# A block of linear attention and a gated feed-forward on one core: the first two token tiles get k and v by direct products, and the schedule's model and order are drawn up anew

## The chip, the cores and the metric

The kernel runs on one core of a Trainium2 chip. The metric is device microseconds of one execution. Of the engines, TensorE is called PE below, VectorE DVE, ScalarE ACT, GpSimd POOL, and SP is the queue that issues nearly all DMAs.

## The reference

`x` has 2048 tokens of 512 elements. It is normalised per token (mean and variance). On the result `xn` two things are computed and multiplied:

```python
qkv = xn @ wqkv                                  # 32 heads of 16
pq, pk = q @ w_phi, k @ w_phi                    # per head, 16 x 16
phi = concat(softmax(p), softmax(-p))            # for q and for k
kv, z = phi_k^T @ v, sum over tokens of phi_k    # per head
s = (phi_q @ kv) / (phi_q . z + 1e-6) @ wo
h = xn @ w1 + b1                                 # 512 -> 1792
g = silu(mish(h) @ w2)                           # 1792 -> 512
out = x + s * g
```

## The kernel before

Tokens are handled in 16 tiles of 128; two tiles form a pair `c` (0 to 7). Every value is float32. A matmul takes each operand as a high half (rounded, written by ACT) and a low half (the rest, by DVE or POOL), so one product costs three matmuls per 128 rows of depth: `lo x hi`, `hi x lo`, `hi x hi`. With 256 rows, a product (`blocks`) is six matmuls.

The large products are cut into 2 x 2 blocks and done with seven block products in place of eight (`SUMS`, `kv_a` to `kv_d`, `q_proj`, `product`). For k and v of a pair, the left blocks are the two tiles and the two halves of the 512 features, the right blocks are k weights and v weights. The seven products need sums and differences of the blocks on both sides: of x (`xs`, split into `fh`/`fl` numbers 107 to 114 for pairs 0 to 3) and of the weights (`ws2`, `ws3`, `ws4` and the `wk` halves). Products of one pair are added in the PSUM tiles `kx`, `kz`, `ky`, and DVE adds the parts in SBUF (`plus`). The k weights are first folded with `w_phi` on PE (`fold`, tiles `wkf`); the same is done for q (`wqf`).

The parts of the program, by the letter that stands in `ORDER`: `N` a tile's normalisation and transposition (`pt`), `Ka` to `Kd` k and v of a pair with the softmax, `A` the sum over tokens (`kvp`, 64 narrow matmuls of a pair), `P` and `M` the weights w1 (prepared and written to DRAM; read back as `w1b`), `F` the first feed-forward product, `L` the reading back of x blocks of the second half (`fh`, `fl` from `xd`), `Q` q, `D` the denominators, `U` the numerators (`pn`), `O` wo, `R` w2, `G` the second feed-forward product (`y`), `E` and `H` the end. Small letters are weights: `wv`, `wq`, `wo`, and `kl`, `ks`, `kd`, `k4` (in the change also `kh`) the parts of the k weights and their sums with those of v. In `D`, `ez` and `tz` are the products with the sum of phi_k and their sums; `put` writes a part of the hidden layer to DRAM (`hd`).

The order on PE is that of `ORDER`. The order on the other engines and on SP comes from a simulation in the kernel's own Python code (`Program.simulate`): it walks through time with a cost per operation, gives every ready operation to a free engine by due time, and holds back those that find no free buffer. There are 38 large buffers (`SLOTS`), 15 small ones (`S2`) and 8 PSUM banks. All instructions are recorded by one helper and so have one line in the profile, L371.

At the start PE runs 13 matmuls on ones (`wake`), and then waits for the first tokens.

Of the kernel before, what the change touches and what calls it, by code (L numbers as in the profile page):

```python
# [23 lines left out]
FC = F // P  # L24
NB = FC // 2
NQ = NT // 2
DIRECT = 0
NC = 8
PEN, HOLD, MARGIN, GUARD = 0, 300, 1000, 140
BACK, COLD, DRATE, LANES, SWITCH = 1500, 3400, 400, 8, 300  # L30
BLOCK, HEAD, FETCH, IDLE = 256, 89, 5200, 2100
BEGIN = {"PE": 1100, "V": 900, "G": 2300, "A": 800, "Q": 800}

# [1 line left out]
SLACK, AHEAD, LAT = 15000, 40000, 150  # L35
WAKE, EACH, NEAR = 13, 2, 4000
ORDER = """
N0 kl wv1 wv0 kd N2 N1 N8 Ka1 wq0 N3 Ka4 ks N9 N6 k4 N7 Ka0 N4 Kb0 N5 Kc0 Kd0 Ka3 Kb1 N10 Kc1 P0 N11 Kb3 Kd1 Ka5 b1
Ka2 A0 Kb2 Kc2 Kc3 A1 Kd2 Fa0 Kd3 Fb0 Fc0 Kb5 N14 Kc5 P4 Kb4 A2 Fa4 Fd0 Kc4 N12 Kd4 N13 P3 N15 Kd5 A3 Fb4 Ka6 Fc4 Ka7
Kb7 Kc7 Kb6 Kc6 Fd4 P2 Fa3 Fb3 wq1 P5 Kd7 Kd6 Fa2 A4 Fa5 Fc3 Fb2 Fc2 P1 Fd3 A5 A6 wQ Fb5 Fc5 Q0 P6 A7 Fd5 Q1 z Fa6 D0  # L40
D1 Fd2 Fa1 Fb1 Fb6 Fc1 D2 Q3 Q2 L M4 Fa11 M5 D3 Fc6 D4 M3 D5 D6 Fb11 Fd1 Fa10 Fc11 Fd6 Q5 Q4 Fb10 Fc10 Fd11 wo1 M6 D8
Fd10 D7 D9 Fa12 M1 Fb12 Fa8 Fc12 Fa13 Fd12 D10 Q7 Fb13 D11 Fb8 Fc13 M0 Ub0 Fc8 Fd13 Fd8 wo0 Q6 Fa7 Ua0 Fb7 M2 Fa9 D12
Fc7 Fb9 D13 O2 O1 Fd7 Fc9 O6 O7 O0 O3 D14 D15 O4 R0 Ub1 R1 Fd9 O5 Ua1 G7 R2 G8 O11 O8 G9 R4 R5 O10 G0 R3 G1 G2 G10 R6
G3 G4 G5 G11 G12 G13 E1 G6 O9 G35 E0 O13 G36 O15 O12 G37 O14 G38 G28 G29 G30 G39 G31 G32 G40 H1 G41 E5 G33 G34 G21 G22
G23 E4 G24 H5 G25 G26 G27 E3 G42 G43 G14 G15 G16 H0 G17 H3 G44 G18 G45 G19 G20 G46 G47 G48 E6 H6 H4 E2 G49 H2 E7
"""
ACT_SET = {AF.Exp: 1, AF.Silu: 3, AF.Mish: 2}

# [5 lines left out]
class Program:  # L54
# [8 lines left out]
    @staticmethod  # L63
    def cost(e, m, a, k):
        aps = [v for v in a if isinstance(v, bass.AP)]
        n = aps[0].free_size()
        if e == "PE":
            if m == "transpose":
                return 109
            n, c = aps[2].free_size(), aps[1].free_size()  # L70
            if aps[1].dtype == F32R:
                return max(n / 2.4 + 0.104 * c, c * 0.835 + 2)
            full = 2 * max(n / 1.2 + 2.5, c * 0.835)
            if aps[1].shape[0] == 32:
                return max(0.146 * n, 24)
            return max(full * aps[0].shape[0] / P, 27)
        if e == "Q":
            return 450
        if e == "A":
            return (60 if aps[1].space == "PSUM" else 110) + 0.833 * n + 93 * sum(isinstance(v, bass.AP) for v in k.values())  # L80
        psum = any(v.space == "PSUM" for v in aps[1:])
        nn = max(v.free_size() for v in aps)
        if e == "V":
            if m == "reciprocal":
                return 70 + 6.3 * n
            if m in ("tensor_scalar", "tensor_copy") and not psum:
                return 70 + 0.52 * n
# [104 lines left out]
    def simulate(self, at):  # L192
# [49 lines left out]
        def go(o, e):  # L242
            nonlocal aset, dma, half, code, fetched, cold
            dur, calls = o.impl[e]
            if e == "A":
                for s in o.sets:
                    if s != aset:
                        dur += 1283
                        aset = s
            if e == "PE":  # L250
                if now > busy["PE"] + IDLE or pe[0].start is None:
                    cold = now + COLD
                if now < cold:
# [12 lines left out]
            if e in o.lock:
                port["V"], port["G"] = now + dur, now + dur + (GUARD if e == "V" else 0)
            o.start, o.eng = now, e
            for n in o.new:
                free[self.tag[n]] -= 1  # L270
                want[self.tag[n]].remove(n)
            busy[e] = now + dur
            end = now + dur + (200 if e == "PE" else 140)
            if e == "Q":
                if not lanes:
                    dur = 0
                    busy[e] = now
                dma = max(dma, now + (1100 if now > 2500 else 1350)) + volume(calls[0][1]) / DRATE
                end = dma + 1150
                lanes.append(end)  # L280
                heapq.heappush(events, (dma - BACK, 2, -1))
            for s in o.succ:
                s.open -= 1
                s.soon = max(s.soon, end)
                if s.open == 0 and s.ndep > 0 and len(s.impl) == 1 and "PE" not in s.impl:
                    for e2 in s.impl:
                        soon[e2].append(s)
            heapq.heappush(events, (now + dur, 2, -1))
            heapq.heappush(events, (end, 1, o.idx))
# [8 lines left out]
        while left:  # L298
# [8 lines left out]
            for kind, i in todo:  # L307
# [6 lines left out]
                elif kind == 1:  # L314
                    o = ops[i]
                    left -= 1
                    for n in o.tiles:
                        if n in uses:
                            uses[n] -= 1
                            if uses[n] == 0:  # L320
                                free[self.tag[n]] += 1
                    for s in o.succ:
                        s.ndep -= 1
                        if s.ndep == 0:
                            s.ready = now
                            if "PE" not in s.impl:
                                for e in s.impl:
                                    heapq.heappush(ready[e], (s.late + (PEN if e == "V" and len(s.impl) > 1 else 0), s.idx))
# [60 lines left out]
def volume(aps):  # L389

    runs = []
    for v in aps[:2]:
# [22 lines left out]
def block_kernel(ctx: ExitStack, tc: tile.TileContext, x, wqkT, wv, phi, wo, w1, b1, w2, out):  # L415
# [120 lines left out]


    xd = dram.tile([P, 2, 7, 2, 4, P], F32, name="xd")
    xc, pts, tiles, fx = {}, {}, {}, {}
# [29 lines left out]
    def norm(t):  # L569
# [25 lines left out]
        split(pt[:, 2:4], *xc[c][2])  # L595
        x12 = alloc("s2", [P, 2, P], f"xr{c}")
        d = slot([P, 4, 2, P], f"xs{c}")
        copy(x12, pt[:, 0:2])
        for i, a, b in ((0, x12, p0[:, 0:2]), (1, pt[:, 2:4], d[:, 0]), (2, pt[:, 2:4], x12), (3, p0[:, 2:4], d[:, 1])):
            V.tensor_tensor(d[:, i], a, b, op=ALU.subtract)  # L600
# [33 lines left out]
    def plus(t, ps):  # L634
        V.tensor_tensor(t, t, ps, op=ALU.add)

    def blocks(ps, lhs, rhs, first):
        with one():
            for k in range(2):
                (ah, al), (bh, bl) = lhs(k), rhs(k)  # L640
                for i, (u, v) in enumerate(((al, bh), (ah, bl), (ah, bh))):
                    PE.matmul(ps, u, v, start=first and k == 0 and i == 0, stop=k == 1 and i == 2, skip_group_check=True)

    kvp = bank([P, 4, 64], "kvp")
    zacc = slot([P, 2 * D], "zacc")
# [5 lines left out]
    def k_soft(t, p, ps):  # L651
# [2 lines left out]
        scale(e, r)  # L654
        ek[t] = e.rearrange("p h s d -> p (h s d)")

    def kv_a(c):
        x, z = bank([P, D], f"kx{c}"), bank([P, D], f"kz{c}")
        v0 = vs[2 * c] = s2(f"v{2 * c}")
        kv_mm(x, c, 0, 0, True)  # L660
# [3 lines left out]
        kv[c] = x  # L664

    def kv_b(c):
        x, y, k1 = kv[c], bank([P, D], f"ky{c}"), s2(f"k{2 * c + 1}p")
        v1 = vs[2 * c + 1] = s2(f"v{2 * c + 1}")
        kv_mm(x, c, 4, 4, False)
# [3 lines left out]
        kv[c] = x, y, k1  # L673

    def kv_c(c):
        x, y, k1 = kv[c]
        kv_mm(x, c, 5, 5, False)
        plus(k1, x)
# [357 lines left out]
    def low_k():  # L1036
        wkv[2] = halves("wk", 1)
        for j in range(2):
            split(fold(wkT, "wk", 2 + j), *(t[:, j] for t in wkv[2]))

    def diff_k():
        t = slot([P, 2, D], "ws3")
        for j in range(2):
            V.tensor_tensor(t[:, j], wraw["v", 0][:, j], fold(wkT, "wk", j), op=ALU.subtract)
        wkv[5] = split_raw(t, "ws3")

    def last_k():
        t = slot([P, 2, D], "ws4")
# [36 lines left out]
    def sums():  # L1085
# [16 lines left out]
        for i in range(4):  # L1102
# [3 lines left out]
    wqT = [None] * KC  # L1106
    wkT = load_wT(KC, "wk", 0, 2) + load_wT(KC, "wk", 1, 2)
    parts = {"b1": bias, "z": sums,
             "ks": sum_k, "kl": low_k, "kd": diff_k, "k4": last_k, "wv": weights_v, "wq": weights_q, "wQ": sums_q, "wo": weights_o, "N": norm, "Ka": kv_a, "Kb": kv_b, "Kc": kv_c, "Kd": kv_d, "A": kv_acc, "Q": q_proj, "D": den, "Ua": num_a, "Ub": num_b,
             "O": att_out, "L": load_g, "P": prep1, "M": again1, "R": prep2,  # L1110
             "Fa": ffn1a, "Fb": ffn1b, "Fc": ffn1c, "Fd": ffn1d, "G": ffn2, "E": final, "H": gate}
    for c in ORDER.split():
# [36 lines left out]
```

## Time and profile before

| what | value |
|---|---|
| median of 3 runs | 502.48 us (501.42 to 505.03) |
| the profiled execution | 501.77 us, span 499.9 us |
| PE busy | 485.1 us, 97%, 3842 matmuls |
| DVE, ACT, POOL busy | 456.0, 287.3, 266.2 us |
| granted PE clock, mean | 0.999 |
| DMA | 105.70 MB, 211 GB/s |

A profile is read from the whole to the piece: busy shares of the engines, then the same by stretches of time, then what the engine that is the bound has waited for, and the chain of work that ended last, in order of time. Names stand as out<-in; in those views the number behind a name is left out, in the order below it is kept.

### The profile page before, as it was taken

To read this page: it belongs to the slowest core of one execution; us is meant where nothing else is said; L and a number is where in the kernel's file an instruction comes from. 1 tells how busy PE (TensorE), PEld (TensorE's weight loads), DVE (VectorE), ACT (ScalarE), POOL (GpSimd) and SP (SyncE) were. 2 spreads that over 40 slices of the span, in tenths; PEclk is the share of its full clock that TensorE was granted. 3 is DMA by queue.
4 is the path that set the end of the run, shared out by engine and by line. 5 is a ranking of instruction groups with operands and counts; after the bars stand their busy time and mean duration, and the time that the engine had idled before them with its cause. 6 is when DMAs were issued, how large, how long until landed. Compare 5 with 4: busy or idle time off the path is not lost.

```text
span 499.9 us, 10373 instructions
## 1 busy us (share of the span) xinstructions
PE 485.1 (97%) x3842; PEld 428.0 (86%) x3842; DVE 456.0 (91%) x883; ACT 287.3 (57%) x440; POOL 266.2 (53%) x199
## 2 busy tenths in 40 slices
PE   6889999999999999998999999999999999999996
PEld 6778888888878979787887888788998999999996
DVE  5999999989899999988988989979998999998985
ACT  3887625564456373332533564587669686876731
POOL 2678999799791567877876398370003403220001
PEclk9999999999999999999999999999999999999999
DMA  8534444368987569997683945573437555676442
GB/s 290 183 109 148 179 129 134 128 224 281 345 329 278 211 215 302 370 366 272 201 272 129 313 150 197 207 234 106 128 115 262 200 171 197 211 258 208 158 140 107
DMA packets 68642, 105.70 MB, mean 211 GB/s; under 512 B 6896, under 2 KB 37744, under 8 KB 68592
## 3 DMA queue, kind: packets, MB, share of 16 engines
q1 hardware_dynamic: 68448, 104.79, 61.4%
q8 instruction: 30, 0.49, 0.4%
q10 hardware_dynamic: 144, 0.26, 0.1%
q14 instruction: 20, 0.16, 0.1%
HBM read 60.60 MB, written 44.43 MB: 210 GB/s over the span
## 4 chain that ended last, share of the span: by engine, by line
PE 82%; DMA 7%; DVE 7%; issue 2%; ACT 1%; POOL 1%; SPq 0%; DVEq 0%; POOLq 0%
PE y L371 21%; PE fx L371 15%; PE pw L371 9%; PE kx L371 9%; PE fy L371 7%; PE ky L371 4%; PE fz L371 4%; PE qx L371 3%; PE pn L371 2%; DMA r<-hd 2%; DMA fl<-xd 2%; PE kz L371 2%; DVE al L371 2%; DMA w1b<-w1d 2%; PE kvp L371 2%
## 5 line engine op out<-in xcount | busy, mean ns | idle before, releaser
L371 ACT ACTIVATE ah<-r 128x896 fp32r<-128x896 f32 x56 | 51.2, 944 | 13.7 <-DVE r L371 9.7
L371 DVE TENSOR_TENSOR al<-r,ah 128x896 fp32r<-128x896 f32 x48 | 52.6, 1123 | 3.0 <-ACT ah L371 2.4
L371 DVE TENSOR_TENSOR r<-r 128x128 f32<-128x128 f32 (+1 forms) x151 | 48.2, 365 | 4.2 <-ACT r L371 3.6
L371 PE MATMUL y<-w2h,al 128*128 128x256 f32 x160 | 45.5, 284 | 0.7 <-DVE yc L371 0.7
L371 PE MATMUL y<-w2h,ah 128*128 128x256 f32 x160 | 45.3, 283 | 0.0
L371 PE MATMUL y<-w2l,ah 128*128 128x256 f32 x160 | 45.3, 283 | 0.0
L371 POOL TENSOR_TENSOR r<-r 128x128 f32<-128x128 f32 (+1 forms) x17 | 9.4, 560 | 63.0 <-DVE r L371 51.2
L371 ACT ACTIVATE r<-r 128x512 f32<-128x512 f32 x56 | 33.6, 624 | 14.7 <-DMA r<-hd 14.3
L371 PE MATMUL y<-w2t,ah 128*128 128x256 f32 x224 | 40.9, 283 | 0.0
L371 PE MATMUL fx<-fh,w1b 128*128 128x512 f32 x112 | 38.9, 394 | 1.3 <-DMA w1b<-w1d 1.3
L371 PEld LDWEIGHTS y<-w2t,ah 128*128 128x128 f32 x224 | 34.9, 192 | 0.0
L371 PEld LDWEIGHTS y<-w2h,al 128*128 128x128 f32 x160 | 30.7, 192 | 1.5 <-DVE yc L371 0.9
L371 PE MATMUL y<-w2t,al 128*128 128x256 f32 x112 | 31.7, 283 | 0.0
L371 PEld LDWEIGHTS y<-w2l,ah 128*128 128x128 f32 x160 | 30.7, 192 | 0.2
L371 PEld LDWEIGHTS y<-w2h,ah 128*128 128x128 f32 x160 | 30.7, 192 | 0.0
L371 PE MATMUL y<-w2g,ah 128*128 128x256 f32 x160 | 30.4, 283 | 0.0
L371 POOL TENSOR_TENSOR xx<-sr,xx 128x512 f32<-128x512 f32 x3 | 3.9, 1299 | 47.7 <-DVE sr L371 41.9
L371 POOL TENSOR_TENSOR al<-r,ah 128x896 fp32r<-128x896 f32 x8 | 17.0, 2130 | 22.7 <-DVE sr L371 18.6
L371 PEld LDWEIGHTS fx<-fh,w1b 128*128 128x128 f32 x112 | 21.0, 188 | 7.0 <-DMA w1b<-w1d 1.5
L371 PEld LDWEIGHTS y<-w2g,ah 128*128 128x128 f32 x160 | 24.9, 192 | 0.0
L371 PE MATMUL y<-w2g,al 128*128 128x256 f32 x80 | 22.6, 283 | 0.0
L371 ACT ACT_TABLE_LOAD x13 | 16.7, 1283 | 9.3 <-DVE yy L371 5.2
(728 smaller groups left out, 1749.7 us busy)
## 6 DMA issues: line engine op xcount, KB each, us to landing
r<-hd SPq DMA_DIRECT2D x56, 256.0 KB, 4.1
xd<-xc SPq DMA_DIRECT2D x8, 896.0 KB, 4.4
w1b<-w1d SPq DMA_DIRECT2D x14, 512.0 KB, 6.7
w1b<-w1d SPq DMA_DIRECT2D x14, 384.0 KB, 5.9
so<-so SPq DMA_DIRECT2D x16, 256.0 KB, 2.7
x<-x SPq DMA_DIRECT2D x15, 256.0 KB, 5.5
w1a<-w SPq DMA_DIRECT2D x7, 512.0 KB, 4.5
w1d<-w1sh SPq DMA_DIRECT2D x7, 512.0 KB, 2.6
```

Source lines behind the costliest of these rows:

```text
L371: ins = getattr(e, m)(*a, **k)
```

## The change

Four things change.

1. Pair 0 (`FRONT = 1`) computes v and k of its two tiles by direct products (`direct`): eight products in place of seven, in four PSUM tiles `kj`, each with two products. It takes x as it is, not sums; for that the first feature half of the second tile gets high and low halves of its own (`xh`, `xl`), and the first half of the k weights too (`high_k`, whose folds are those that `diff_k` had).
2. The model of the schedule gets a read latency of DMAs (`READ`, `WRITE`), a DMA delay at each fetch of instructions (`STALL`), and a PE operation is ready 110 ns after its last input (`AHEAD_PE`). `BACK`, `SWITCH` and the price of narrow matmuls change.
3. `ORDER` is another one throughout.
4. Line numbers move: the recording helper is L375.

```diff
-DIRECT = 0
+DIRECT, FRONT = 0, 1
-BACK, COLD, DRATE, LANES, SWITCH = 1500, 3400, 400, 8, 300
+BACK, COLD, DRATE, LANES, SWITCH = 2650, 3400, 400, 8, 361
+READ, WRITE, STALL, AHEAD_PE = 1150, 150, 1500, 110
...
-N0 kl wv1 wv0 kd N2 N1 N8 Ka1 wq0 N3 Ka4 ks N9 N6 k4 N7 Ka0 N4 Kb0 N5 Kc0 Kd0 Ka3 Kb1 N10 Kc1 P0 N11 Kb3 Kd1 Ka5 b1
+wv0 N0 wv1 kl N4 N1 wq0 N2 N3 ks b1 Ka0 Kb0 kh N5 Ka2 k4 N6 Kd0 P0 N7 Kc0 kd Ka1 Kb1 wq1 N8 Kb2 N9 Ka3 Kc1 Kd1 Kc2 Fa0
...
+                    dma = max(dma, at) + STALL
...
-                dma = max(dma, now + (1100 if now > 2500 else 1350)) + volume(calls[0][1]) / DRATE
-                end = dma + 1150
+                dma = max(dma, now + (1100 if now > 2500 else 1350) + (READ if reads(calls[0][1]) else WRITE))
+                dma += volume(calls[0][1]) / DRATE
+                end = dma
...
+        if c < FRONT:
+            x12_[c] = tuple(alloc("s2", [P, 2, P], f"x{u}{c}", F32R) for u in "hl")
+            split(pt[:, 0:2], *x12_[c])
...
+    def direct(c, i):
+        t, ps = 2 * c + i % 2, bank([P, D], f"kj{c}{i}")
+        lhs = [xc[c][0], xc[c][1]] if t % 2 == 0 else [x12_[c], xc[c][2]]
+        for j, (a, (h, l)) in enumerate(zip(((0, 1), ("k", 2))[i // 2], lhs)):
+            blocks(ps, lambda k: (h[:, k], l[:, k]), lambda k: tuple(t[:, k] for t in wkv[a]), j == 0, j == 1)
+        if i < 2:
+            vs[t] = s2(f"v{t}")
+            copy(vs[t], ps)
+            return
+        k = s2(f"k{t}p")
+        copy(k, ps)
+        k_soft(t, k, ps)
...
+    def high_k():
+        wkv["k"] = halves("wk", 0)
+        t = wraw["d"] = slot([P, 2, D], "ws3")
+        for j in range(2):
+            ps = fold(wkT, "wk", j)
+            split(ps, *(u[:, j] for u in wkv["k"]))
+            V.tensor_tensor(t[:, j], wraw["v", 0][:, j], ps, op=ALU.subtract)
```

How instructions move, at three places. The first is DVE's beginning (BN_STATS is a tile's statistics, `nb` and `rs` belong to its normalisation, x_141 and x_144 are the first tile). Before:

```order
L371 BN_STATS st_142<-x_141 128x6
L371 BN_AGGR mv_140<-st_142 128x2
L371 TENSOR_SCALAR rs_139<-mv_140 128x1
L371 TENSOR_TENSOR phit<-phic,bmask 128x512
L371 BN_STATS st_163<-x_162 128x6
L371 BN_AGGR mv_161<-st_163 128x2
L371 TENSOR_SCALAR nb_143<-mv_140,rs_139 128x1
```

and of the change:

```order
L375 BN_STATS st_145<-x_144 128x6
L375 BN_AGGR mv_143<-st_145 128x2
L375 BN_STATS st_158<-x_157 128x6
L375 TENSOR_SCALAR rs_142<-mv_143 128x1
L375 BN_STATS st_160<-x_159 128x6
L375 BN_STATS st_166<-x_165 128x6
L375 TENSOR_SCALAR nb_146<-mv_143,rs_142 128x1
L375 TENSOR_TENSOR phit<-phic,bmask 128x512
```

The statistics of three other tiles now stand ahead of `nb_146`, which the first tile waits for (before, those of one), and the mask product `phit` now stands behind it. On SP the loads of x_157 and x_159 now stand ahead of phic, then x_165, and only then the first two wkT.

The second place is PE's first products (`wkf`, `wqf` folds; `pt` transposes). Before:

```order
L371 MATMUL pt_183<-ident,x_178 128x128 x4
L371 MATMUL kx_185<-wv0h,fl_102 128x512
...
L371 MATMUL kz_186<-wv1h,fl_104 128x512
...
L371 MATMUL wqf_190<-phit,wqT_188 128x128 x4
L371 MATMUL wqf_191<-phit,wqT_188 128x128 x4
L371 MATMUL pt_193<-ident,x_164 128x128 x4
L371 MATMUL kx_196<-wv0h,xc_184 128x512
```

and of the change:

```order
L375 MATMUL wkf_193<-phit,wkT_138 128x128 x4
L375 MATMUL kj_196<-wv0h,fl_102 128x512
...
L375 MATMUL kj_196<-wv1h,fl_104 128x512
...
L375 MATMUL kj_198<-wv0h,xl_172 128x512
...
L375 MATMUL kj_198<-wv1h,fl_106 128x512
...
L375 MATMUL wkf_203<-phit,wkT_135 128x128 x4
L375 MATMUL wkf_204<-phit,wkT_136 128x128 x4
L375 MATMUL pt_206<-ident,x_159 128x128 x4
```

All folds for the weight sums (`wkf_192`, `wkf_193`) and half of wq's now stand ahead of the first product; then come the two pairs of v products of pair 0 and the folds of the first half of the k weights. Behind these stand pt_206, one product each of kx and kz, pt_222, and then kj_223, the first k product. kj_196 is written into the PSUM bank that wkf_154 had, kj_198 into that of pt_168.

The third place is SP's order where the x blocks are read back (`w1d` and `xd` are in DRAM). Before:

```order
L371 DMA kvw<-kvd 32x4x256
L371 DMA fh_607<-xd 128x1024
L371 DMA fl_608<-xd 128x1024
...
L371 DMA kvw<-kvd 32x4x256
L371 DMA w1b_621<-w1d_350 128x768
L371 DMA kvw<-kvd 32x4x256
L371 DMA w1b_622<-w1d_351 128x768
L371 DMA fh_609<-xd 128x1024
```

and of the change:

```order
L375 DMA w1b_532<-w1d_365 128x768
L375 DMA w1d_554<-w1ah_550 128x768
L375 DMA w1b_533<-w1d_366 128x768
L375 DMA hd_506<-hc_503 128x512
L375 DMA w1b_534<-w1d_367 128x1024
L375 DMA kvd<-kvf 128x256
L375 DMA hd_506<-hb_502 128x512
L375 DMA w1b_535<-w1d_368 128x1024
...
L375 DMA fh_617<-xd 128x1024
L375 DMA fl_618<-xd 128x1024
```

The four w1b loads that the first new products need now stand ahead of the first x block, in the rows of `kvd`; before, they stand behind it. On PE the `kvp` matmuls stand in five groups (two of 64, three of 128) where before they stand in seven (six of 64, one of 128).

More of the change, by code (lines that the diff above doesn't have):

```diff
@@ L37 @@
 ORDER = """
-N0 kl wv1 wv0 kd N2 N1 N8 Ka1 wq0 N3 Ka4 ks N9 N6 k4 N7 Ka0 N4 Kb0 N5 Kc0 Kd0 Ka3 Kb1 N10 Kc1 P0 N11 Kb3 Kd1 Ka5 b1
[L39 to L45, printed above, removed]
+wv0 N0 wv1 kl N4 N1 wq0 N2 N3 ks b1 Ka0 Kb0 kh N5 Ka2 k4 N6 Kd0 P0 N7 Kc0 kd Ka1 Kb1 wq1 N8 Kb2 N9 Ka3 Kc1 Kd1 Kc2 Fa0
+Kb3 N10 N11 Fb0 Kc3 A0 Fc0 Kd2 Ka4 Kd3 Kb4 Fd0 Ka5 N14 A1 A2 Kc4 A3 Kd4 P4 Fa4 N15 Kb5 Kc5 Kd5 P6 N12 N13 Fb4 P3 Fc4
+Ka7 Ka6 Kb6 P5 Kc6 Kb7 Kc7 Fa6 Kd6 Fa3 Fd4 Fb6 A4 P2 A5 Kd7 Fb3 Fc6 Fc3 Fa2 Fa5 Fb2 Fd3 Fd6 Fc2 A6 wQ A7 Q0 M4 Fb5 z
+Fc5 P1 Fa1 D0 D1 Fd2 Q2 Q1 M6 Q3 D2 L Fb1 Fa11 M3 D3 Fc1 Fd1 Fd5 D4 Fa13 Fb11 Fb13 Fc13 Q4 D5 Fa10 Fc11 Fb10 wo0 Fd11
+M5 Fd13 D6 M2 D8 Fc10 Fd10 D7 Fa12 Q6 Q5 Fa9 Fb12 D9 Fc12 Fd12 D10 D11 Fb9 Ub0 Fc9 D12 Fd9 wo1 M0 D13 M1 Q7 Fa7 Fb7
+Ua0 D14 Fc7 Fa8 Fb8 D15 O3 O5 Fc8 O1 O2 O7 Fd7 O6 R0 Ub1 Fd8 O4 R2 G7 R3 O0 R1 G8 Ua1 G9 R5 G10 O10 O9 O8 O11 G28 R4
+G29 G11 G30 R6 G31 G12 G13 G32 G33 G35 E1 G34 O15 O14 E4 G36 O13 G37 G38 O12 G39 G40 G0 G1 G2 H4 G3 G41 E5 G4 G21 G22
+G5 G6 G23 G24 G25 G26 G42 E0 G27 H1 E3 H0 G43 G44 H5 G14 G15 G45 G16 G17 G46 G18 G19 G47 G20 H3 G48 E6 E2 G49 H6 H2 E7
 """
@@ L74, in cost @@
             if aps[1].shape[0] == 32:
-                return max(0.146 * n, 24)
+                return max(0.155 * n, 24)
             return max(full * aps[0].shape[0] / P, 27)
@@ L323, in simulate @@
                         s.ndep -= 1
-                        if s.ndep == 0:
+                        if s.ndep == 0 and "PE" in s.impl:
+                            heapq.heappush(events, (now + AHEAD_PE, 0, s.idx))
+                        elif s.ndep == 0:
                             s.ready = now
-                            if "PE" not in s.impl:
-                                for e in s.impl:
-                                    heapq.heappush(ready[e], (s.late + (PEN if e == "V" and len(s.impl) > 1 else 0), s.idx))
+                            for e in s.impl:
+                                heapq.heappush(ready[e], (s.late + (PEN if e == "V" and len(s.impl) > 1 else 0), s.idx))
             if pos < len(pe) and busy["PE"] <= now and pe[pos].ready >= 0 and fits(pe[pos]):
@@ L399, in volume, with reads @@
     return aps[0].free_size() * aps[0].shape[0] * (4 if min(runs) > 128 else 4.7)
+def reads(aps):
+    return "DRAM" not in str(aps[0].space).upper()
 def bcast(a):
@@ L538, in block_kernel @@
     xd = dram.tile([P, 2, 7, 2, 4, P], F32, name="xd")
-    xc, pts, tiles, fx = {}, {}, {}, {}
+    xc, x12_, pts, tiles, fx = {}, {}, {}, {}, {}
     def blocks_x(q):
@@ L635, in plus, with blocks @@
         V.tensor_tensor(t, t, ps, op=ALU.add)
-    def blocks(ps, lhs, rhs, first):
+    def blocks(ps, lhs, rhs, first, last=True):
         with one():
@@ L641, in blocks @@
                 for i, (u, v) in enumerate(((al, bh), (ah, bl), (ah, bh))):
-                    PE.matmul(ps, u, v, start=first and k == 0 and i == 0, stop=k == 1 and i == 2, skip_group_check=True)
+                    PE.matmul(ps, u, v, start=first and k == 0 and i == 0, stop=last and k == 1 and i == 2, skip_group_check=True)
     kvp = bank([P, 4, 64], "kvp")
@@ L655, in k_soft @@
         ek[t] = e.rearrange("p h s d -> p (h s d)")
+    def direct(c, i):
[10 more added lines that the diff above has]
+        k_soft(t, k, ps)
     def kv_a(c):
+        if c < FRONT:
+            return direct(c, 0)
         x, z = bank([P, D], f"kx{c}"), bank([P, D], f"kz{c}")
@@ L666, in kv_b @@
     def kv_b(c):
+        if c < FRONT:
+            return direct(c, 1)
         x, y, k1 = kv[c], bank([P, D], f"ky{c}"), s2(f"k{2 * c + 1}p")
@@ L675, in kv_c @@
     def kv_c(c):
+        if c < FRONT:
+            return direct(c, 3)
         x, y, k1 = kv[c]
@@ L683, in kv_d @@
     def kv_d(c):
+        if c < FRONT:
+            return direct(c, 2)
         x, y, k1 = kv.pop(c)
@@ L1039, in low_k @@
             split(fold(wkT, "wk", 2 + j), *(t[:, j] for t in wkv[2]))
+    def high_k():
[5 more added lines that the diff above has]
+            V.tensor_tensor(t[:, j], wraw["v", 0][:, j], ps, op=ALU.subtract)
     def diff_k():
[L1042 to L1045, printed above, removed]
+        wkv[5] = split_raw(wraw["d"], "ws3")
     def last_k():
@@ L1108, in block_kernel @@
     parts = {"b1": bias, "z": sums,
-             "ks": sum_k, "kl": low_k, "kd": diff_k, "k4": last_k, "wv": weights_v, "wq": weights_q, "wQ": sums_q, "wo": weights_o, "N": norm, "Ka": kv_a, "Kb": kv_b, "Kc": kv_c, "Kd": kv_d, "A": kv_acc, "Q": q_proj, "D": den, "Ua": num_a, "Ub": num_b,
+             "ks": sum_k, "kl": low_k, "kh": high_k, "kd": diff_k, "k4": last_k, "wv": weights_v, "wq": weights_q, "wQ": sums_q, "wo": weights_o, "N": norm, "Ka": kv_a, "Kb": kv_b, "Kc": kv_c, "Kd": kv_d, "A": kv_acc, "Q": q_proj, "D": den, "Ua": num_a, "Ub": num_b,
              "O": att_out, "L": load_g, "P": prep1, "M": again1, "R": prep2,
```

## The prediction

> **What bounds the kernel now.** I cut the span into stages first, to see where TensorE (PE) is not busy. Columns: the stretch and its length, then busy time and number of instructions of PE, of PE's weight loads, of DVE, ACT and POOL, the granted clock, DMA share, GB/s.
>
> ```profile
> core 0: us, PE busy (x) PEld busy (x) DVE busy (x) ACT busy (x) POOL busy (x), PEclk, DMA share, GB/s
> 0.00:10.00 10.00, 6.97 (x46) 6.59 (x46) 4.51 (x13) 3.08 (x4) 1.68 (x10) 1.00 0.76 261
> 10.00:30.00 20.00, 16.16 (x108) 13.98 (x108) 18.95 (x56) 15.36 (x30) 11.37 (x12) 1.00 0.64 213
> 30.00:36.00 6.00, 5.12 (x26) 3.83 (x27) 5.98 (x16) 5.73 (x12) 6.00 (x4) 1.00 0.00 0
> 36.00:200.00 164.00, 164.00 (x1279) 137.04 (x1278) 155.51 (x265) 87.06 (x133) 128.22 (x87) 1.00 0.65 224
> 200.00:232.00 32.00, 30.00 (x178) 26.29 (x177) 29.30 (x58) 10.66 (x19) 23.50 (x16) 1.00 1.00 375
> 232.00:470.00 238.00, 238.00 (x2007) 215.86 (x2006) 218.71 (x442) 156.95 (x233) 94.09 (x72) 1.00 0.58 193
> ...
> 495.50:499.90 4.40, 0.00 (x0) 0.00 (x0) 1.27 (x3) 0.42 (x1) 0.00 (x0) 0.89 0.18 61
> ```
>
> PE is the bound. From 36 us it is busy without a gap, but for 2.0 us between 200 and 232, under 1 us in the piece left out (470 to 495.5), and the last 4.4 us, in which only the last output is finished. Before 36 us it is idle for 3.0 + 3.8 + 0.9 = 7.7 us, and there DVE is the busy engine (18.95 of 20 us). So an edit can win in the first 36 us, in the 2.0 us of the middle, or by changing PE's own work, and nowhere else. The list of PE's waits names the causes (total us, times, longest):
>
> ```profile
> engine line waited for: us in total, times, longest us
> PE pt L371 <- ACT x L371: 3.0, 2, 1.8
> PE wkf L371 <- DMA wkT<-wqkT: 1.7, 2, 1.4
> PE fx L371 <- DMA w1b<-w1d: 1.3, 1, 1.3
> ...
> PE pt L371 <- DVE wsl L371: 1.0, 1, 1.0
> ...
> PE fy L371 <- DMA fl<-xd: 0.7, 1, 0.7
> ```
>
> All sums go against the profiled execution: 501.77 us, of which the span is 499.9. The median of the three runs, 502.48, is 0.7 higher.
>
> **Added PE work: +1.36 us.** Prices of PE's pieces, from the chain of waits (start, us, what):
>
> ```profile
> 25.33 3.59 PE wkf L371 x32
> 44.47 1.36 PE kz L371 x6
> 101.86 0.87 PE pt L371 x8
> ```
>
> A fold pass costs 0.11 us, a product of six 512-column matmuls 1.36, a pair of token transposes 0.87. Pair 0 takes eight products in place of seven: one more. It has no cover, since PE is full. The high and low halves of the k weights need no new folds: high_k takes the two that diff_k had. They cost two ACT copies and two DVE subtractions more, and xl/xh one each; pair 0 loses three DVE additions (k1, v0, v1). DVE's total in the first stage is thus about the same; its order is what counts.
>
> **The start: -2.8 us.** I compare the moment at which both kernels have done the same PE work. Before, PE starts the first ws2 product here (start, us, engine, instruction):
>
> ```profile
> 35.56 0.48 PE L371 MATMUL kx<-ws2h,fl 128*128 128x512 f32 x1
> ```
>
> By then it has done 64 fold passes of wk, 16 of wq, six products and nine token transposes. After the change PE reaches kj_223 (the first k product) with the same folds, six products (kj_196 and kj_198 are two each, then one kx and one kz) and seven transposes. Two transposes are 0.87, so before's moment is 34.7.
>
> When does kj_196 start? The bank that it writes is that of wkf_154, and the second row "wkl_152" on DVE frees it; that row stands 34 instructions behind the statistics of x_165. The chain of waits shows DVE's steps in just this stretch:
>
> ```profile
> 2.66 5.53 DMA x<-x
> 8.21 1.33 DVE st L371 x2
> ...
> 11.61 0.33 DVE fl L371
> ...
> 12.32 0.91 DVE x L371 x2
> 13.23 0.60 DVE ws L371
> 13.82 1.13 DVE wv0l L371
> 14.96 0.12 DVE nb L371
> ```
>
> The fifth 256-KB load was at hand at 8.2 us and DVE had waited for it. In the new order x_165 is the fourth such load, so I take 7.5 us and 0.7 for its statistics: 8.2. Then 14 small rows at 0.1, six 512-column ones at 0.60, three normalisations at 0.46, wv0l at 1.13 and ten of 256 columns at 0.33 make 10.8: 19.0 us. DVE also waits there for ACT, whose copy wv0h now comes after three loads more (wqT among them), and whose copies of wqf stand between those of pt. No row of before shows these waits. Their bounds are nothing, and 4.7 us: the 3.0 and 1.0 us that PE lost to ACT and to DVE in the list above, and 0.7 if x_165 lands only at 8.2. I take 2.0, between them. **kj_196 starts at 21.0 us (19.0 to 23.7).** From there PE needs 6 x 1.36 + 16 x 0.11 + 0.87 = 10.8 and is at kj_223 at 31.8. It is then at 31.8 where it was at 34.7: 2.9, and 0.1 off for the restarts after transposes gives 2.8. With the bounds it is 4.8 down to 0.1.
>
> Hidden at no cost: x_144 is normalised later. Before, from its nb to its transposes (start, us, engine, instruction):
>
> ```profile
> 6.39 0.18 DVE L371 TENSOR_SCALAR nb<-mv,rs 128x1 f32<-128x1 f32 x1
> 7.47 0.66 PE L371 MATMUL pt<-ident,x 128*128 128x128 f32 x4 [1.83 <-ACT x L371]
> ```
>
> Now nb_146 stands behind x_165's statistics, at 8.2 us, so the transposes come near 9.3 instead of 7.5. PE has no product to do until the wv splits are there, so this wait takes the place of the later ones on wkT, 1.7 us. Were the splits early, it would cost 1.7.
>
> **Fewer switches: -0.7 us.** PE's kvp groups alone and in a double:
>
> ```profile
> 141.44 1.03 PE kvp L371 x64
> 142.47 1.59 PE fx L371 x6
> ...
> 154.94 1.93 PE kvp L371 x128
> 156.87 1.58 PE fx L371 x6
> ```
>
> Two single groups with their next products take 2 x (1.03 + 1.59) = 5.24; a double with one such product and an ordinary one 1.93 + 1.58 + 1.36 = 4.87. A merger saves 0.37. Before there are seven groups, after there are five: two mergers, 0.7.
>
> **The middle: -0.8 us.** The two waits at 210 and 230 us end so:
>
> ```profile
> 200.45 9.81 DMA fl<-xd
> ...
> 219.46 2.42 POOL ez L371
> 221.91 1.23 DVE tz L371
> 223.16 8.48 DMA w1b<-w1d
> ```
>
> The first is a queue that is full: 375 GB/s in that stretch, and PE needs fl_614 as it lands. In the new order the four w1b loads of M4 stand ahead of the x loads, and 21 narrow products (three rounds of Q) and two wide ones that need none of the new blocks lie between the first x load and the first use. I take this wait, 0.7 with its restart 0.1, as gone; bounds 0 and 0.8. The second is a chain over POOL and DVE (den's ez, tz) that frees a slot for w1b. After, w1b_639 waits for such a tz too, with PE's fx_678 behind it. I leave its 1.4 as it is; bounds: gone, or double.
>
> **Sum:** 501.77 + 1.36 - 2.8 - 0.7 - 0.8 = 498.8. Runs scatter round their median, and that of before is 0.7 over its profiled run; half of this on top gives **499.2 us**.
>
> **A rule weighed.** PE idles 1.8 us ahead of its first transposes before; the wake-up matmuls thus end near 5.7, and after the change it would idle to 9.3, 3.6 us. The wake-up matmuls show what a slow clock costs:
>
> ```profile
> 1.10:3.30 2.20, 2.18 (x10) 2.19 (x11) 1.00 0.40 142
> 3.30:5.50 2.20, 2.20 (x18) 2.16 (x17) 1.00 1.07 335
> ```
>
> In equal stretches PE does 10 passes, then 18. If it falls back for as long as it took to wake (from 1.1 to about 3.3 us), it loses about 1 us, and up to 1.5 in 3.4 us. That is a rival, below. The Trainium skill, "TensorE: Matmul & The Clock Gate", section "Part 1: The HAM clock gate", says that PE drops to half rate after an idle window of about 3.4 us and needs a busy one to come back, and that the window runs free. By that rule the new gap is at the limit; the trace agrees on the waking, and the granted clock column, 1.00 in both stretches, doesn't show it.
>
> **Rivals.**
>
> *The start wins more and the middle clears.* x_165 lands at 6, DVE doesn't wait, and w1b's wait goes too: 501.77 + 1.36 - 4.5 - 0.7 - 2.1 gives 495.8; with some of this 496.4. For: DVE's steps leave 19.0. Against: all must go well.
>
> *The win is given back.* DVE and POOL stay full (5.98 and 6.00 of 6 us at 30 to 36) and the same splits are due, so PE waits later, for ws3l or the k copies, 1.5 to 2 us: 500.9. For: POOL has ws2l, ws4l, ws3l and the first FFN weights in a row. Against: these are needed later than before, behind four k products.
>
> *Slower: the bank.* One mechanism: kj_196 and then kj_198 wait for DVE to free wkf_154's and pt_168's banks. Each us that the second wkl_152 ends after 21.0 costs one, and break-even with before is 21.0 + 2.9 = 23.9. At 25.1 (x_165 at 8.2, ACT waits of 4, and 1.4 more where POOL's wv1l holds DVE up) the time is 503.3. For: DVE is the bound of this stage already. Against: it must lose more than any wait listed above.
>
> *The clock falls back:* at most 1.5 us on the forecast, 500.7, less what PE would wait anyway.
>
> That the change doesn't do what it says is no rival here: the order shows kj and the counts.
>
> **Chances.** Forecast 0.47 (its own range 497.6 to 500.6), more won 0.17, given back 0.19, bank 0.12, clock 0.05. Against 502.48, 1% is 5.0 us: about what a measurement of this kernel tells from no change. Below 497.5 lies most of "more won" and the forecast's edge: 0.17. Above 507.5 lies only a tail of the bank case, 0.03. The rest, 0.80, is within 1%. The range takes in most of the cases on both sides: 496.0 to 503.2.
>
> **What would show it.** First transposes near 9.3 us; kj_196 at 21 and kj_223 near 32; no PE wait between kj_196 and 50 us; five kvp groups; no wait on fl<-xd near 210, one of 1 to 2 us on w1b near 225; PE's busy time up by about a microsecond at most. Wrong if kj_196 starts past 23, if PE waits more than 1 us for DVE or POOL between 32 and 60, or if a new DMA wait stands after 232 us, where the order has changed everywhere and I counted nothing.

## The result, and the profile after

The changed kernel takes **495.76 us** (median of 4 runs, 495.69 to 496.87), the kernel before 503.11 beside it (501.42 to 505.03): a ratio of 0.9872, 95% interval 0.983 to 0.9915. The forecast was 499.2; the time lies 0.2 us below the low end of its range, and put on the 502.48 us that the forecast was made against, the ratio gives 496.0, that low end itself. The profiled execution took 495.69 us, its span 494.0: 5.9 us less span than before.

The same cut by stretches as before (PE, weight loads, DVE, ACT, POOL, clock, DMA):

```profile
0.00:10.00 10.00, 6.62 (x34) 6.43 (x35) 5.52 (x19) 2.48 (x3) 2.90 (x12) 0.92 0.84 278
10.00:30.00 20.00, 19.62 (x132) 17.99 (x132) 18.87 (x51) 16.75 (x35) 13.88 (x13) 0.96 0.63 205
30.00:36.00 6.00, 6.00 (x32) 4.92 (x31) 5.70 (x17) 6.00 (x13) 4.84 (x6) 1.00 0.38 154
36.00:200.00 164.00, 163.34 (x1290) 137.88 (x1289) 156.57 (x270) 87.42 (x132) 116.94 (x76) 1.00 0.67 232
200.00:232.00 32.00, 32.00 (x162) 27.33 (x161) 30.04 (x55) 12.92 (x19) 25.04 (x17) 1.00 0.92 320
232.00:470.00 238.00, 238.00 (x2046) 217.62 (x2045) 224.49 (x448) 158.88 (x237) 90.33 (x73) 1.00 0.60 199
```

In the first 36 us PE is now idle for 3.4 + 0.4 = 3.8 us in place of 7.7, and between 200 and 232 not at all. All of PE's waits (us, times, longest):

```profile
PE pt L375 <- ACT x L375: 2.3, 1, 2.3
PE wake L375 <- DVE mhalf L497: 1.1, 1, 1.1
PE fx L375 <- POOL w1sl L375: 0.7, 1, 0.7
PE wkf L375 <- ACT wqf L375: 0.4, 1, 0.4
```

The waits for wkT, fl, w1b, wsl and yc are gone; one for w1sl, at 105 us, is new. PE's start, row by row:

```profile
1.12 4.98 PE L375 MATMUL wake<-ones 128*128 128x128 f32 x26 [1.12 <-DVE mhalf L497]
8.36 1.11 PE L375 MATMUL pt<-ident,x 128*128 128x128 f32 x4 [2.26 <-ACT x L375]
9.26 3.14 PE L375 MATMUL wkf<-phit,wkT 128*128 128x128 f32 x16
...
16.32 3.84 PE L375 MATMUL wkf<-phit,wkT 128*128 128x128 f32 x32 [0.38 <-ACT wqf L375]
19.91 0.48 PE L375 MATMUL kj<-wv0h,fl 128*128 128x512 f32 x1
...
30.84 0.48 PE L375 MATMUL kj<-wkh,fl 128*128 128x512 f32 x1
```

kj_196 starts at 19.91 without a wait, and kj_223 at 30.84. Sixteen fold passes take 3.14 us here, while the 32 further down take 3.84: the first ones ran at half rate.

### The profile page after: what moved, and what is told of

Same layout as the page of the kernel before. It is cut to its first block, busy times and chain, and to the rows that moved or that the text cites. A ratio compares the mean times of both kernels' runs of the same rounds, so it can differ in the third digit from the quotient of the medians.

```text
span 494.0 us, 10391 instructions
## 1 busy us (share of the span) xinstructions
PE 485.1 (98%) x3848; PEld 431.5 (87%) x3848; DVE 456.0 (92%) x885; ACT 290.2 (59%) x446; POOL 255.2 (52%) x194
## 4 chain that ended last, share of the span: by engine, by line
PE 93%; POOL 2%; DVE 2%; DMA 1%; ACT 1%; issue 1%; SPq 1%; POOLq 0%; DVEq 0%
PE y L375 29%; PE fx L375 15%; PE pw L375 9%; PE fy L375 8%; PE kx L375 7%; PE qx L375 5%; PE fz L375 4%; PE ky L375 3%; PE qy L375 2%; PE kj L375 2%; PE pn L375 2%; PE kz L375 2%; PE kvp L375 1%; PE qz L375 1%; PE wkf L375 1%; DMA x<-x 1%
## 5 line engine op out<-in xcount | busy, mean ns | idle before, releaser
L375 ACT ACTIVATE ah<-r 128x896 fp32r<-128x896 f32 x56 | 51.4, 945 | 17.4 <-DVE r L375 14.1
L375 DVE TENSOR_TENSOR al<-r,ah 128x896 fp32r<-128x896 f32 x52 | 56.2, 1105 | 2.4 <-ACT ah L375 1.4
L375 DVE TENSOR_TENSOR r<-r 128x256 f32<-128x256 f32 (+1 forms) x145 | 44.1, 344 | 1.9 <-ACT r L375 1.1
L375 PE MATMUL y<-w2h,al 128*128 128x256 f32 x160 | 45.4, 284 | 0.0
L375 PE MATMUL y<-w2l,ah 128*128 128x256 f32 x160 | 45.3, 283 | 0.0
L375 PE MATMUL y<-w2h,ah 128*128 128x256 f32 x160 | 45.3, 283 | 0.0
L375 POOL TENSOR_TENSOR r<-r 128x128 f32<-128x128 f32 (+1 forms) x23 | 12.5, 556 | 59.6 <-DVE al L375 28.4
L375 PE MATMUL y<-w2t,ah 128*128 128x256 f32 x224 | 41.0, 283 | 0.0
L375 PE MATMUL fx<-fh,w1b 128*128 128x512 f32 x112 | 38.8, 393 | 0.0
L375 ACT ACTIVATE r<-r 128x512 f32<-128x512 f32 x56 | 33.6, 624 | 7.9 <-DMA r<-hd 6.5
L375 PEld LDWEIGHTS y<-w2t,ah 128*128 128x128 f32 x224 | 35.0, 192 | 0.0
L375 PE MATMUL y<-w2t,al 128*128 128x256 f32 x112 | 31.7, 283 | 0.0
L375 PEld LDWEIGHTS y<-w2h,al 128*128 128x128 f32 x160 | 30.7, 192 | 0.6 <-issue 0.4
L375 PEld LDWEIGHTS y<-w2l,ah 128*128 128x128 f32 x160 | 30.7, 192 | 0.2
L375 PEld LDWEIGHTS y<-w2h,ah 128*128 128x128 f32 x160 | 30.7, 192 | 0.0
L375 PE MATMUL y<-w2g,ah 128*128 128x256 f32 x160 | 30.4, 283 | 0.0
L375 POOL TENSOR_TENSOR xx<-sr,xx 128x512 f32<-128x512 f32 x2 | 2.6, 1293 | 51.5 <-DVE xx L375 37.6
L375 PEld LDWEIGHTS fx<-fh,w1b 128*128 128x128 f32 x112 | 21.0, 188 | 5.4 <-issue 1.2
L375 PEld LDWEIGHTS y<-w2g,ah 128*128 128x128 f32 x160 | 25.0, 192 | 0.0
L375 PE MATMUL y<-w2g,al 128*128 128x256 f32 x80 | 22.7, 283 | 0.0
L375 PE MATMUL fx<-fl,w1b 128*128 128x512 f32 x56 | 21.9, 390 | 0.0
```

The lines of the kernel that those rows point to most:

```text
L375: ins = getattr(e, m)(*a, **k)
```

## The experiments

### Undoing or adding one part, with an order made for another program

Four kernels mixed the change's three parts (direct products, model, order). `r_` and `e_` names are labels of runs.

```text
 e_seven       DIRECT, FRONT = 0, 0; new model; new ORDER with "kd Kc0 P0 N7 Kd0" for "Kd0 P0 N7 Kc0 kd"
 e_directonly  DIRECT, FRONT = 0, 1; old model; old ORDER with "wv0 kh kd" for "wv0 kd"
 e_newmodel    DIRECT, FRONT = 0, 0; new model; old ORDER with "wv0 kh kd" for "wv0 kd"
 e_oldmodel    DIRECT, FRONT = 0, 1; old model; new ORDER
```

> The change with its new model and its new order, but pair 0 by seven products as before (kd and Kc0 stand ahead of Kd0, as seven products need; the spare halves of the k weights are left out). Theory A, that the direct products give PE early work that needs no sums: PE has 1.4 us less to do but waits 2 to 4 us for sums of pair 0 before 40 us, so 497 to 499 us. Theory B, that the order and the model win alone and the direct products only cost their 1.4 us: no new wait before 40 us and 494 to 495 us.

> The kernel before with its old model and its old order, and only pair 0 by direct products (kh stands ahead of kd). Theory A: in the old order pair 0's v and k stand after pair 1's and 4's, so the direct products come too late to fill the first 25 us; 1.4 us more work and about the same waits: 502 to 505 us. Theory C, that the direct products are enough by themselves: at least 2 us faster than before, 500 us or less.

> The kernel before with its old order of PE and seven products, and only the new model, which moves the work on DVE, ACT, POOL and SP (kd in two steps, kh and kd, as in the change). Theory A, that PE's order carries the gain: within 1.5 us of before, 500 to 504 us. Theory D, that the model is what wins (it places loads and splits better, so the waits on fl, w1b and yc go): 497 to 499 us.

> The change with its new order and its direct products, and the old model. Theory A: most of the gain stays, as PE's order is the same: 496 to 499 us, with one or two waits of about 1 us that the new model had avoided. Theory D, that the model is what wins: 500 to 503 us.

| run | median, us | ratio to before (95%) | PE's longest wait |
|---|---|---|---|
| e_seven | 520.38 | 1.0366 (1.029 to 1.0442) | 13.2 us, at 124 |
| e_directonly | 525.01 | 1.0457 (1.039 to 1.0523) | 11.4 us, at 106 |
| e_newmodel | 537.99 | 1.0721 (1.0653 to 1.0789) | 11.5 us, at 98 |
| e_oldmodel | 522.78 | 1.0412 (1.0347 to 1.0478) | 10.9 us, at 98 |

Every expectation failed by 19 us or more, whichever theory it came from. In all four the largest loss is one wait of `pt` on ACT's normalised x. In e_newmodel, DVE's rows (start, us):

```profile
66.49 1.22 DVE L375 BATCH_NORM_STATS2 st<-x 128x6 f32<-128x512 f32 x2
...
89.15 1.22 DVE L375 BATCH_NORM_STATS2 st<-x 128x6 f32<-128x512 f32 x2
90.50 0.90 DVE L375 TENSOR_SCALAR rs<-mv 128x2 f32<-128x2 f32 x2
91.31 1.21 DVE L375 TENSOR_TENSOR zacc<-zacc,k4e 128x1024 f32<-128x1024 f32 x1
...
97.20 0.33 DVE L375 TENSOR_SCALAR nb<-mv,rs 128x1 f32<-128x1 f32 x2 [0.82 <-POOL rs L375]
```

and PE's, where it ends:

```profile
98.31 1.12 PE L375 MATMUL pt<-ident,x 128*128 128x128 f32 x4 [11.53 <-ACT x L375]
```

The statistics of two tiles are done at 67.7 us, but the next step, `rs` on two elements per partition, stands in DVE's order behind 23 us of other work, and four additions of `zacc` stand between it and `nb`. So no transfer is late, the planned order is. Why the plan does this is argued from the code, not shown on the chip: it gives DVE no such operation while POOL runs, and POOL's longest gap between 67 and 91 us is 1.45 us.

What follows: a program, a model and an order that were not fitted to one another lose 17 to 35 us. These runs therefore don't price a part.

### The parts, each with an order searched for it

Next, each combination got an order of its own: entries of `ORDER` were moved about at random, one by one, and moves were kept that shortened the kernel's own plan and replays of it with durations stretched a little. Products and model are as named; the only other edit is `ORDER` (without direct products, the spare halves of the k weights are left out as well).

```text
 r_newseven, r_newseven2    FRONT = 0, new model; two searches
 r_olddirect, r_olddirect2  FRONT = 1, old model; two searches
 r_newdirect                FRONT = 1, new model; a search from the changed kernel
```

> The new model's constants and formulas, but seven products for the first two tiles as before (no direct products), and an order of its own: the entries of the order moved about one by one, keeping every move that shortened the kernel's own plan and four of its replays with slightly stretched durations. Theory M (the gain comes from a model that stands closer to the chip, with an order fitted to it): as fast as the changed kernel, 492 to 496 us. Theory P (the gain comes from the direct products, which need fewer weights before the first product): no better than 498 to 501 us, the start some 3 us later than in the changed kernel.

> The direct products with the old model's constants and formulas, and an order of its own, found by the same search under the old model. Theory M: the chip doesn't keep to such a plan, waits of 1 us and more come back for loads and for DVE: 499 to 504 us. Theory P: 494 to 498 us.

> The changed kernel with its order searched further in the same way; nothing else is changed. If the order was already as good as the model can tell: 495 to 497 us. If the changed kernel's three waits ahead of 105 us (2.3, 0.7 and 0.4 us) can be ordered away: 493 to 495 us. If a plan's gain of 1 us isn't kept by the chip: 496 us or above.

> As r_newseven (new model, seven products for the first two tiles, no direct products), with another order that the same search found from another sequence of random moves. If the new model is what counts: 494 to 498 us, as r_newseven's 496.9. If each order's own luck counts for as much (as r_newdirect's 499.7 against the changed kernel's 495.8 lets one suspect): anywhere from 495 to 503 us.

> As r_olddirect (direct products, old model), with another order that the same search found from another sequence of random moves. If the new model is what counts: 500 to 505 us, as r_olddirect's 503.0. If each order's own luck counts for as much: anywhere from 495 to 503 us, and as likely ahead of r_newseven2 as behind it.

| run | median, us | ratio to before (95%) | PE idle, 0 to 36 us | 100 to 300 |
|---|---|---|---|---|
| before | 501.4 to 503.4 | 1 | 7.75 | 2.0 |
| changed kernel | 495.76 | 0.9872 (0.983 to 0.9915) | 3.76 | 0.66 |
| r_newseven | 496.88 | 0.9907 (0.987 to 0.9944) | 4.84 | 1.07 |
| r_newseven2 | 500.28 | 0.9978 (0.9953 to 1.0002) | 3.69 | 3.49 |
| r_newdirect | 499.66 | 0.9956 (0.9928 to 0.9984) | 4.43 | 1.31 |
| r_olddirect | 502.98 | 1.0022 (0.9995 to 1.005) | 2.40 | 4.44 |
| r_olddirect2 | 517.07 | 1.0288 (1.0249 to 1.0328) | 5.11 | 1.93 |

**The direct products aren't needed for most of the gain.** r_newseven has none, its interval overlaps that of the changed kernel, and its profiled span, 495.2, has 4.7 of the 5.9 us; PE's idle time at its start is down by 2.9 of the 4.0 us. Its 496.88 us lie between the two forecasts, 0.9 above theory M's range and 1.1 below theory P's. **Nor are they enough.** r_olddirect starts best of all and gives everything back. Its stretches (0 to 36, 100 to 200, 200 to 300 us):

```profile
0.00:36.00 36.00, 33.60 (x211) 29.73 (x212) 29.91 (x84) 26.14 (x51) 23.45 (x29) 1.00 0.64 217
...
100.00:200.00 100.00, 98.07 (x742) 83.04 (x740) 95.17 (x156) 52.32 (x78) 61.48 (x39) 1.00 0.77 268
200.00:300.00 100.00, 97.49 (x738) 82.13 (x737) 93.85 (x177) 42.93 (x73) 76.81 (x47) 1.00 0.67 244
```

and its largest waits, all behind the start:

```profile
PE qx L371 <- DVE q13p L371: 2.1, 1, 2.1
PE qx L371 <- ACT q1p L371: 1.4, 1, 1.4
```

**That the model is what counts is not shown either.** r_newseven and r_newseven2 differ in nothing but the order, and lie 3.4 us apart with intervals that don't touch, so that only the forecast "each order's own luck" takes in both; a longer search made r_newdirect 3.9 us slower than the kernel it began with. r_newseven2 lost its good start here:

```profile
PE fx L375 <- DMA w1b<-w1d: 1.6, 1, 1.6
PE pw L375 <- DVE ol L375: 1.4, 1, 1.4
```

r_olddirect2 missed both of its forecasts for a reason of its own: more than ten output blocks are left to its last 20 us. But even its PE ends only near 495 us, and r_olddirect's at 494; under the new model PE ends at 489.5 us in the changed kernel and 490.8 in r_newseven, but at about 494 in the other two. So neither of two orders under the old model was good, and two of four under the new one; that is too few to settle it. What stays open is how much of the 5.9 us is the new model's and how much one lucky order's; an order is worth some 3 to 4 us either way.

### More wake matmuls

```diff
+MORE = 9
...
+                if m == "matmul" and a[0].tensor.name.startswith("wake"):
+                    self.woken = getattr(self, "woken", 0) + 1
+                    if self.woken == WAKE:
+                        for _ in range(MORE):
+                            getattr(e, m)(*a, **k)
```

The 13 wake matmuls are 26 passes in the profile, the 9 more are 18.

> The changed kernel with 9 more wake matmuls behind the 26 at the start and every other instruction in the same order, so that PE has no idle 2 us ahead of its first transposes. Theory hidden: the half-rate passes from 8.4 to 11.6 us run beside ACT's and DVE's first steps, which set the start of kj_196; kj_196 stays within 0.3 us of 19.9 us, and the time within 0.4 us of the changed kernel's. Rival clock: the 16 wkf passes of 213 ns run at 112 ns, kj_196 starts 1 to 1.6 us earlier, and the time falls by as much.

496.52 us, 0.991 (0.9879 to 0.9941), span 493.9: the time of the changed kernel (its span is 494.0; the medians differ by 0.8 us, within the 495.66 to 498.6 of these runs). PE's rows:

```profile
8.82 1.95 PE L376 MATMUL wkf<-phit,wkT 128*128 128x128 f32 x16
...
15.92 3.84 PE L376 MATMUL wkf<-phit,wkT 128*128 128x128 f32 x32 [1.55 <-ACT wqf L376]
19.51 0.48 PE L376 MATMUL kj<-wv0h,fl 128*128 128x512 f32 x1
```

The passes run at full rate, PE is 1.6 us ahead at 11.6 us, and then waits 1.55 us in place of 0.38 for ACT's copy of wqf. kj_196 starts 0.40 us earlier, a little outside the 0.3 of theory hidden; in the next run, whose start is that of the changed kernel, PE is at this point 0.45 us earlier without more wake matmuls. So theory hidden holds in the main, and the row names the gate: ACT.

Of these 0.40 us little arrives. At 39.4 us PE's next product starts just as POOL's split of `fl` ends,

```profile
38.66 0.76 POOL L376 TENSOR_TENSOR fl<-xs,fh 128x256 fp32r<-128x256 f32 x1
```

```profile
39.44 0.47 PE L376 MATMUL kx<-ws2h,fl 128*128 128x512 f32 x1
```

at 39.42; in the changed kernel this split ended at 39.06, well ahead of PE. From there PE is 0.11 us ahead, and the span is 0.1 us shorter.

### A push at 20 us

```diff
+PUSH = 18
...
+                if i == 0 and o.part == "Ka0" and o.eng == "PE" and "kj" in str(o.writes):
+                    for _ in range(PUSH):
+                        e.matmul(a[0][:, 0:P], *self.dummy, start=True, stop=True)
```

> The changed kernel with 18 more f32 matmuls (36 passes of 112 ns, 4.0 us) that write nothing of use, ahead of the first of its direct products at 19.9 us; every other instruction in the same order. Theory carried (PE is the bound from there to the end, so that a start is worth its time at the end): 3.0 to 4.0 us more, a span of 497.0 to 498.0, where the 0.7 us wait at 105 us is hidden behind the later PE. Rival given back (other engines set the pace somewhere behind, and the earlier start only waits there): under 2 us more.

The condition holds for both products of kj_196, so there are 36 extra matmuls, not 18, and the second set overwrites a part of the first product of tile 0 (the output is wrong; only the time counts here):

```profile
19.46 4.18 PE L378 MATMUL kj<-ones 128*128 128x128 f32 x36
23.40 0.48 PE L379 MATMUL kj<-wv0h,fl 128*128 128x512 f32 x1
...
24.88 4.18 PE L378 MATMUL kj<-ones 128*128 128x128 f32 x36
28.82 0.48 PE L379 MATMUL kj<-wv1h,fl 128*128 128x512 f32 x1
```

Each set holds PE for 3.94 us, 7.9 in all; the span is 501.7, 7.7 longer, and the time 504.38 us. Matched matmul by matmul, PE is 7.43 us behind the changed kernel at its next product and 7.76 behind at 246 us. Theory carried holds, for twice the push: a microsecond lost at 20 us is one at the end. What it said of the wait on w1sl doesn't: it isn't hidden behind the later PE, but comes again, 0.68 us long, at 112 us.

### One exchange on POOL

```diff
+        k = next(o for o in ops if o.part == "Kc4" and o.eng == "G" and any(n.startswith("k9e") for n in o.writes))
+        s = next(o for o in ops if o.part == "P4" and o.eng == "G" and any(n.startswith("w1sl") for n in o.writes))
+        ops.remove(k)
+        ops.insert(ops.index(s) + 1, k)
...
```

> The changed kernel with two neighbours on POOL exchanged near 101 us, every other instruction in the same order: the split of w1 (w1sl, 2.39 us) goes ahead of the scaling k9e<-k9e,k9r (1.94 us), whose result is read at 138 us. ACT ends w1sh at 101.0 us, so w1sl should end at 103.4 us instead of 104.95. Theory release (POOL alone sets PE's 0.7 us wait at 105 us): the wait goes, the span falls by 0.5 to 0.8 us, to 493.2 to 493.5. Rival next: PE meets the later zacc, k8e or w1 of the next part within 10 us instead, and the span stays at 493.8 to 494.2.

496.24 us, 0.9878 (0.9834 to 0.9921), span 494.5. The changed kernel's POOL, and the PE row that waits for it:

```profile
100.66 1.94 POOL L375 TENSOR_TENSOR k9e<-k9e,k9r 128x1024 f32<-128x1024 f32 x1
102.56 2.39 POOL L375 TENSOR_TENSOR w1sl<-w1s,w1sh 128x1024 fp32r<-128x1024 f32 x1
```

```profile
105.00 0.50 PE L375 MATMUL fx<-fh,w1sl 128*128 128x512 f32 x1 [0.66 <-POOL w1sl L375]
```

and after the exchange:

```profile
101.33 2.42 POOL L382 TENSOR_TENSOR w1sl<-w1s,w1sh 128x1024 fp32r<-128x1024 f32 x1 [0.41 <-ACT w1sh L382]
103.70 1.94 POOL L382 TENSOR_TENSOR k9e<-k9e,k9r 128x1024 f32<-128x1024 f32 x1
```

```profile
104.32 0.48 PE L382 MATMUL fx<-fh,w1sl 128*128 128x512 f32 x1
...
107.49 0.50 PE L382 MATMUL fx<-fh,w1sl 128*128 128x512 f32 x1 [0.19 <-ACT hb L382]
```

The wait goes and PE, 0.22 us behind the changed kernel from 54 us on, is 0.68 us ahead at 105 us; at 108 it is ahead by 0.24, at 120 behind by 0.08, at 132 by 0.38, in small steps that begin with the wait for hb. So the named wait was POOL's, but the time goes the way of the rival: the span is 0.3 us above even the rival's range. No run was faster than the changed kernel.

## Why the prediction was right or wrong

**The start (-2.8): right in kind, too small.** Against before's 34.7, kj_223 at 30.84 is 3.9 us earlier. DVE's rows show which terms were mis-sized:

```profile
6.65 0.69 DVE L375 BATCH_NORM_STATS2 st<-x 128x6 f32<-128x512 f32 x1 [0.20 <-DMA x<-x]
...
19.03 0.68 DVE L375 TENSOR_TENSOR wkl<-wkf,wkh 128x512 fp32r<-128x512 f32 x1
```

x_165 was there at 6.65 and its statistics done at 7.34, not 8.2. From there to the end of the second wkl, at 19.71, are 12.4 us, where I had 10.8 of steps and 2.0 of waits: nearly right. The step that failed outright is the gate. I let DVE's wkl release kj_196; that bank was free 0.2 us before PE came, and e_wake shows PE waiting for ACT's wqf instead, which starts the last folds at about 16 us whatever PE did before. ACT's rows show what holds this copy back:

```profile
12.81 0.81 ACT L375 ACTIVATE x<-x,nb,rs 128x512 f32<-128x512 f32 x1 [1.00 <-DVE nb L375]
...
15.69 0.58 ACT L375 ACTIVATE wqf<-wqf 128x512 f32<-128x512 f32 x1
```

Between the two ACT works without a gap, on wv0h and wv1h above all, and ahead of them it waited for DVE. Whether the copy of wqf ahead of wv1h would win anything was not run. From kj_196 to kj_223 PE took 10.9 us, as counted (10.8). And this start is not the products' alone: r_newseven gets 2.9 of the 4.0 us of idle time without them, by order and model.

**Hidden transposes: right.** They came at 8.36 rather than 9.3, and e_wake shows that PE had 1.6 us to spare behind them.

**Added product (+1.36) and switches (-0.7): together too dear.** PE's busy time is 485.1 us in both kernels, so the sum's 0.7 us of added work aren't there, although the wake matmuls and the folds of wk take 1.1 us more, at half rate. Counted from the start of each matmul to the next, less idle time, the k and v products take 0.5 us more (for 342 matmuls in place of 336), the first feed-forward products 0.8 less and the kvp groups 0.3 less: 0.5 less in all, where the two terms make 0.7 more. Which restarts of PE this comes from isn't isolated. There are five kvp groups, and the doubles cost what was taken (start, us, from the chain):

```profile
69.29 1.03 PE kvp L375 x64
...
85.95 1.92 PE kvp L375 x128
87.87 1.60 PE kx L375 x6
```

**The middle (-0.8): the w1b step failed.** The fl wait went, as said. The other, which I left at 1.4, went too: PE has all 32.0 us between 200 and 232, 2.0 more than before. I had named "gone" as its bound and kept the value, since the order still has such a tz ahead of the load; but the order doesn't say when that tz comes. The w1b loads came earlier: before, six of them were issued from 218.1 to 223.2 us and landed by 231.6, where PE's wait ends; after, four were issued from 212.4 to 219.2 and landed by 226.9, and PE, which turns to products with w1b at 224.2, doesn't wait. Whether the order or the model brought them forward isn't shown.

**Nothing after 232 us: wrong by 0.7.** Near its end, the kernel before had this wait:

```profile
PE y L371 <- DVE yc L371: 0.7, 1, 0.7
```

It went, and the one on w1sl came, so the two cancel. For what is given back I looked at 32 to 60 us; it came at 105.

Together: the span falls by 5.9 us at an unchanged busy time of PE, since PE is idle 4.0 us less before 36 us and 2.0 less between 200 and 232, and the waits on yc and w1sl cancel. The sum had +0.7 for the work, -2.8 for the start and -0.8 for the middle: all three were too cautious, by 0.7, 1.2 and 1.2 us, and no error hid another. The rival "more won and the middle clears", at 496.4 with 0.17, is what happened, with a start of 4.0 in place of its 4.5 and with waits of DVE (0.48 us for POOL's rs, 0.65 for ACT's wv0h) that it had taken as gone.

**The clock rival: the mechanism came, the cost didn't.** Passes of 213 ns ran from 8.36 to 11.6 us, behind 2.26 us without work and at half the granted clock:

```profile
6.10:8.34 2.24, 0.00 (x0) 0.00 (x0) 2.04 (x9) 0.81 (x1) 0.38 (x1) 1.00 1.05 399
8.34:11.76 3.42, 3.40 (x16) 3.40 (x17) 3.31 (x14) 2.01 (x4) 1.22 (x2) 0.50 1.03 399
```

But ACT's gate hid them: in f_swap, which starts as the changed kernel does, the same 16 fold passes took 1.95 us and not 3.14, and kj_196 began at 19.91 in both. I had also read the waking as over by about 3.3 us; in the kernel before, passes of 213 ns run until 4.0. The rule in the Trainium skill, "TensorE: Matmul & The Clock Gate", section "Part 1: The HAM clock gate", speaks of an idle window of about 3.4 us; here 2.26 us of idle were enough, while 1.83 us in the kernel before were not, and the measurement decides. Nor does the length of the idle time decide alone: e_seven has the same 2.26 us ahead of its first transposes and stays at full rate. That the window runs free of the kernel's start, as the Trainium skill says there, agrees with the traces: the wake matmuls start at 1.12 us in the changed kernel, f_swap and f_push, and full rate comes at 4.93, 6.57 and 7.29 us; and in every trace the changes of rate that follow lie 3.41 us or a multiple of it apart (in the changed kernel at 4.93, 8.34 and 11.76).

## What to carry to other kernels

When a kernel's order has been searched for one program under one plan, a single part of a change can't be priced by undoing it: first give each variant a search of its own, and run two orders of each, since two orders of one program lay 3.4 us apart here. Where PE is full, time lost at the start is carried whole to the end (7.4 us behind at the next product, 7.7 in the span); time won is carried as far as the other engines keep up (0.40 us ahead at 19.5 us, 0.1 in the span). To win it, follow the last release (here ACT's copy), and what that waited for, rather than the busiest engine. And a small wait taken away deep in a full program may come back in pieces within 30 us.

## What the hardware showed that was not expected

An operation of DVE on two elements per partition can take as long as POOL's operation beside it still has to run. In e_seven, DVE's rows of one kind:

```profile
87.37 0.16 DVE L375 TENSOR_SCALAR rs<-mv 128x2 f32<-128x2 f32 x1
...
115.30 1.06 DVE L375 TENSOR_SCALAR rs<-mv 128x2 f32<-128x2 f32 x1
```

and POOL's beside the second:

```profile
113.99 2.34 POOL L375 TENSOR_TENSOR zacc<-zacc,k7e 128x1024 f32<-128x1024 f32 x1
```

It ends at 116.36, POOL's at 116.33. In e_directonly one of 0.90 us ends at 99.27, POOL's zacc at 99.25. This agrees with the Trainium skill, "SBUF — State Buffer", section "SBUF: two separate sides": the port pair that DVE and GpSimd share is locked for a whole instruction, and the other engine waits. The Trainium skill says so there of DVE operations in a two-port mode or with two inputs in SBUF; no run here shows in which mode this one ran.

The length of the idle time doesn't decide whether PE falls to half rate; how its work lies in stretches of 3.41 us, counted from the first rise to full rate, would fit. In the changed kernel PE was busy for 1.2 us of the stretch from 4.93 to 8.34, and half rate followed. In e_seven it was busy for 1.6 us of the one from 4.12 to 7.53, its 2.26 us of idle time reached into the next, and full rate stayed. Where the limit lies between the two, these runs don't show.
